# One row of w4 moved onto a part of the DMA engines, and the x row added on VectorE: a decode kernel on one core

## The chip, the cores and the metric

The kernel runs on one core of one Trainium2 chip. The metric is the device time in microseconds of one execution, the median of several runs. Beside the times there is one profiled execution, taken by the hardware profiler; its span runs from the first to the last instruction of the core and is about 2 us shorter than the time of the same execution.

## The reference, cut to what matters

```python
def _A_ref(x, k_cache, v_cache, wq, wo):           # x: 1 x 1 x 1024, already layer-normed
    q = (x @ wq) as 32 heads of 128
    k, v = 4 cached heads of 65536 keys x 128, each used by 8 query heads
    p = softmax(q k^T * 128 ** -0.5)
    return (p v) as one row of 4096 @ wo            # wo: 4096 x 1024

def _B_ref(x, w1, w2, w3, w4):
    h = gelu(layernorm(x) @ w1)
    hs = concatenate(four quarters of h, each shifted along the sequence) @ w2
    x1 = x + hs
    return x1 + gelu(layernorm(x1) @ w3) @ w4       # w3: 1024 x 3584, w4: 3584 x 1024

xn = layernorm(x)
return x + _A_ref(xn, ...) + _B_ref(xn, ...)
```

The sequence has one position, so every shifted quarter of h is zero; the kernel multiplies w2 with a column of zeros. All inputs are bf16. The two caches are 67 MB each; with the weights some 170 MB are read from HBM for one row of 1024 outputs.

## The kernel before, in words

Everything is a stream of loads through three large SBUF slots (`big`, 128 partitions x 64 KB, `SLOTS = 3`), and `Stream.pump` issues the next load on SyncE's queue (SP) as soon as a slot is free. The order is wq, w3, w1 and w2, then K and V in eight units (four cache heads, two halves each; the last V comes after wo), and at the end w4. A slot is free again when its user calls `st.done`.

For each unit `compute_k` transposes the K tile in place with VectorE (DVE, L361), multiplies it with the queries on TensorE (PE, L366), takes the maximum, lets ScalarE (ACT, L384) form the exponentials, and transposes these with DVE (L387). `compute_v` (L416) multiplies them with V. After the second unit of a cache head `group_rows` (L425 to L447) brings the heads' outputs into columns, and `project` multiplies them with wo.

The result is gathered in the PSUM tile `psB`: partitions 0-31 hold output columns 0 to 511, partitions 32-63 the other half, each row repeated 32 times. `row_acc` (L225) adds one product to it. Into `psB` go, in this order: the x terms (the x row scaled by `ln_s1` and shifted by `ln_s2`, as `accx`, through an identity), the w2 product, the projection of the first three heads (which `project` gathers in a row of PSUM, `copy_projection` at L463 copies to SBUF and `add_projection` adds through an identity), the products of w4 rows, and the projection of the last head.

w4 has 3584 rows, 28 for each partition; the tile `hT` holds in column c the 128 activations for row c of every partition. `W4_PIECES = (8, 12, 5, 2, 1)` gives the rows of each load (L187). The first 8 rows and the 12 of the second load go into `psB` with `compute_w4`: rows 0-2 at once, 3-7 behind the gathering of the last head, the 12 behind the last head's projection. Then ACT copies `psB` to `sums` (L497). The last `NARROW = 8` rows go, with output halves cut into quarters, to two other PSUM tiles (`pm_r`, L504): five rows (`AHEAD`), then `sums` through an identity, then three rows. ACT and DVE cast the two tiles (L520, L521), and ACT issues the store.

The lines around the change that a sentence doesn't say:

```python
copy_projection()
summed = compute_v(NU - 1)
with tc.issue_after(summed):
    add_projection()
early = sum(W4_PIECES[:AT_ONCE])
compute_w4(0, FIRST)
with tc.issue_after(tail["gathered"]):
    compute_w4(FIRST, early)
projected = project(HKV - 1)
with tc.issue_after(projected):
    compute_w4(early, FC - NARROW)
```

Of the kernel before, what the change touches and what calls it, by code (L numbers as in the profile page):

```python
# [8 lines left out]
BF16 = mybir.dt.bfloat16  # L9
F32 = mybir.dt.float32  # L10
ACTF = mybir.ActivationFunctionType
ALU = mybir.AluOpType
# [3 lines left out]
P = 128  # L16
# [3 lines left out]
SLOTS = 3  # L20
W4_PIECES = (8, 12, 5, 2, 1)
FIRST = 3
AT_ONCE = 1
NARROW = 8
AHEAD = 5

# [70 lines left out]
def kernel(  # L97
# [14 lines left out]
    nc = tc.nc  # L112
# [13 lines left out]
    assert DH == P and HQ // HKV == 8 and HKV == 4 and D == 1024 and F == 3584 and S == 1  # L126
    assert SK % UKEYS == 0 and sum(W4_PIECES) == FC
    NB = SK // UKEYS
# [22 lines left out]
    class Stream:  # L151
# [17 lines left out]
        def load(self, it):  # L169
            t = big.tile([P, ROW], BF16, name="big")  # L170
            self.tiles[it] = t
            go = nc.sync.dma_start
            if it == "wq":
                go(out=t[:], in_=A_wq.rearrange("(p c) n -> p (c n)", c=DC))
            elif it == "w3":
                go(out=t[:, 0:DC * F], in_=B_w3.rearrange("(p c) f -> p (c f)", c=DC))
            elif it == "w12":
                go(out=t[:, 0:DC * D], in_=B_w1.rearrange("(p c) n -> p (c n)", c=DC))
                go(out=t[:, DC * D:2 * DC * D], in_=B_w2.rearrange("(m c) n -> m (c n)", c=DC))
            elif it == "wo":  # L180
                go(out=t[:].rearrange("p (g n) -> p g n", g=HKV),
                   in_=A_wo.rearrange("(g p j) n -> p g (j n)", g=HKV, p=P))
            elif it == "w4":
                w4_v = B_w4.rearrange("(m c) n -> m c n", c=FC)
                c0 = 0
                for n in W4_PIECES:
                    go(out=t[:, c0 * D:(c0 + n) * D], in_=w4_v[:, c0:c0 + n, :].rearrange("p c n -> p (c n)"))  # L187
                    c0 += n
            else:
                kind, i = it  # L190
                g, b = divmod(i, NB)
                cache = A_k_cache if kind == "K" else A_v_cache
                go(out=t[:], in_=cache[0, g, b * UKEYS:(b + 1) * UKEYS, :].rearrange("(p ct) d -> p (ct d)", p=P))
# [18 lines left out]
    for b in range(2):  # L212
        nc.gpsimd.tensor_copy(
            out=spread[:, 2 * b:2 * b + 2, :].rearrange("p r (a i) -> p r a i", a=4),
            in_=ident_f[:, 64 * b:64 * b + 64].rearrange("p (i r) -> p r i", r=2).unsqueeze(2).to_broadcast([P, 2, 4, 32]))

    qdiag = const.tile([P, LEAD + 4 * P], BF16, name="qdiag")
    nc.gpsimd.memset(qdiag[:], 0.0)
# [5 lines left out]
    def row_acc(j, lhsT, rhs, start=False):  # L224
        return nc.tensor.matmul(psB[32 * j:32 * j + 32, :], lhsT=lhsT.to_broadcast([lhsT.shape[0], 32]), rhs=rhs, start=start,  # L225
                                stop=False, tile_position=(0, 32 * j), skip_group_check=True)
# [8 lines left out]
    def layernorm(src, tag):  # L235
# [44 lines left out]
    nc.vector.tensor_tensor(out=ln_s2[:], in0=negmean1[:], in1=rstd1[:], op=ALU.mult)  # L280
    accx = ppool.tile([1, D], F32, name="accx", tag="p")
    nc.vector.tensor_scalar(out=accx[:], in0=x_row[0:1, :], scalar1=ln_s1[0:1, 0:1], scalar2=ln_s2[0:1, 0:1],
                            op0=ALU.mult, op1=ALU.add)
    for j in range(2):
        row_acc(j, ident_f[0:1, 0:1], accx[0:1, 512 * j:512 * (j + 1)], start=True)

# [31 lines left out]

    hT = const.tile([P, FC], BF16, name="hT")

    def compute_w3():
# [8 lines left out]
        nc.vector.transpose(out=h_row[:], in_=h_row[:])  # L330
        nc.vector.tensor_copy(out=hT[:], in_=h_row[:, ::32])

    def compute_w12():
# [8 lines left out]
        for c in range(DC):  # L342
            for j in range(2):
                row_acc(j, g_col[:], wt[:, 1, c, 512 * j:512 * (j + 1)])
        st.done("w12")
# [115 lines left out]
    def copy_projection():  # L461
        tail["o"] = st.tiles["w4"][0:1, FC * D:FC * D + 2 * D].bitcast(F32)
        nc.vector.tensor_copy(out=tail["o"].rearrange("p (j n) -> p j n", j=2), in_=tail["rows"][0:1, 0:2, :])  # L463

    def add_projection():
        for j in range(2):
            row_acc(j, ident_f[0:1, 0:1], tail["o"][:, 512 * j:512 * (j + 1)])

# [7 lines left out]
    compute_w3()  # L476
    compute_w12()
    for u in range(NU - 1):
        compute_k(u)
        compute_v(u)  # L480
# [4 lines left out]
    copy_projection()  # L485
    summed = compute_v(NU - 1)
    with tc.issue_after(summed):
        add_projection()
    early = sum(W4_PIECES[:AT_ONCE])
# [4 lines left out]
    with tc.issue_after(projected):  # L494
        compute_w4(early, FC - NARROW)
    sums = ogpool.tile([64, 512], F32, name="sums", tag="og")
    nc.scalar.copy(out=sums[:], in_=psB[0:64, :])  # L497
    quarters = [ps_M.tile([P, 512], F32, name="pm_r", tag="pm") for _ in range(2)]
# [8 lines left out]
    def narrow_rows(lo, hi, start=False):  # L507
        wt = st.tiles["w4"]
        for c in range(lo, hi):
# [3 lines left out]

    narrow_rows(FC - NARROW, FC - NARROW + AHEAD, start=True)
    quarter_acc(lambda j: ident_f[0:64, 32 * j:32 * j + 1].to_broadcast([64, 32]),
                lambda j, h: sums[:, 256 * h:256 * (h + 1)])
    narrow_rows(FC - NARROW + AHEAD, FC)

# [34 lines left out]
```

## Time and profile before

| what | value |
|---|---|
| time, median of 7 runs | 400.90 us (400.78 to 401.01) |
| profiled execution: time, span | 400.86 us, 398.8 us |
| read from HBM | 169.87 MB, 426 GB/s over the span |
| busy: PE, DVE, ACT, GpSimd (POOL) | 230.8, 209.5, 27.6, 5.4 us |
| data queue (q1), share of 16 engines' span | 98.9% |
| w4's five loads issued on SP | 361.70 to 363.93 us of the span |
| last w4 load landed, last matmul begins | 396.60, 396.64 us |

The page of a profile gives busy time by engine, the granted TensorE clock and the DMA share in 40 slices, the DMA queues, and the chain of work that ended last. The chain and the timeline count microseconds from the start of the span. A line of the timeline has start, duration, engine, program line, operation, output and inputs with shapes, the count of merged instructions, and in brackets the idle time of the engine ahead of it with what ended it. Beside these views the trace keeps each DMA packet with its queue, start, duration and size, and each increment of a DMA's semaphore; it doesn't name the engine of a packet.

### The profile page before, as it was taken

How to read it: one execution, taken by the hardware profiler on the slowest of the kernel's cores; microseconds unless marked ns; L12 is line 12 of the kernel's file. 1: busy time of each engine (PE TensorE's matmuls, PEld its weight loads, DVE VectorE, ACT ScalarE, POOL GpSimd, SP SyncE). 2: the span in 40 equal slices, each digit the busy share in tenths (PEclk: the TensorE clock that was granted, in tenths of full speed). 3: DMA queues.
4: the chain of work that ended last, by engine and by line, in shares of the span. 5: the costliest groups of instructions: out<-in, count | busy, mean ns of one | idle time of the engine just before them, and what ended most of it. 6: DMA issues, size and time to landing. Idle time of an engine off the chain costs nothing.

```text
span 398.8 us, 2595 instructions
## 1 busy us (share of the span) xinstructions
PE 230.8 (58%) x1372; PEld 45.2 (11%) x878; DVE 209.5 (53%) x155; ACT 27.6 (7%) x36; POOL 5.4 (1%) x28
## 2 busy tenths in 40 slices
PE   0461960591569247833974286429543945394995
PEld 0210000000200110011001100101010102010132
DVE  0620010974196559643953696269449932894140
ACT  1001010003000200020002000200110010002000
POOL 2000000000000000000000000000000000000000
PEclk9996896697769587966695679678966886599999
DMA  9998999999999999999999999999999999999996
GB/s 421 421 443 380 440 440 480 440 421 421 416 428 427 421 480 442 421 421 427 427 429 427 460 454 416 421 421 434 440 429 447 447 427 388 417 450 442 406 428 254
DMA packets 4144, 170.03 MB, mean 426 GB/s; under 512 B 419, under 2 KB 421, under 8 KB 678
## 3 DMA queue, kind: packets, MB, share of 16 engines
q1 hardware_dynamic: 4128, 169.87, 98.9%
q8 instruction: 9, 0.15, 0.1%
q14 instruction: 1, 0.01, 0.0%
q10 hardware_dynamic: 6, 0.00, 0.0%
HBM read 169.87 MB, written 0.00 MB: 426 GB/s over the span
## 4 chain that ended last, share of the span: by engine, by line
DMA 56%; DVE 21%; PE 17%; ACT 2%; another core or an unknown queue 2%; issue 1%; SPq 0%; DVEq 0%; ACTq 0%
DMA big<-in_A_k_cache_dram 42%; DVE big L361 15%; PE sc L366 11%; DMA big<-in_B_w_dram 8%; DMA big<-in_A_wq_dram 5%; PE oacc L416 4%; DVE p_sb L387 2%; DVE mx L371 2%; ACT p_sb L384 2%; PE psq L291 1%; SPq L187 0%; PE pm_mx L373 0%; DVE m L375 0%; PE pm_mx L380 0%
## 5 line engine op out<-in xcount | busy, mean ns | idle before, releaser
L366 PE MATMUL sc<-big,qdiag 128*128 128x512 bf16 x512 | 130.5, 417 | 65.2 <-DVE big L361 59.5
L361 DVE STREAM_TRANSPOSE big<-big 128x4096 f32<-128x4096 f32 x32 | 139.4, 4412 | 50.5 <-DMA big<-in_A_k_cache_dram 50.5
L416 PE MATMUL oacc<-big,p_sb 128*32 128x512 bf16 x512 | 43.0, 510 | 34.5 <-DVE p_sb L387 34.5
L371 DVE TENSOR_REDUCE mx<-sc 128x1 f32<-128x2048 f32 x8 | 18.3, 2292 | 30.5 <-PE sc L366 30.5
L366 PEld LDWEIGHTS <-qdiag 128*128 128x128 bf16 x128 | 13.3, 104 | 177.9 <-issue 146.6
L384 ACT ACTIVATE p_sb<-sc,nball 128x2048 bf16<-128x2048 f32 x8 | 15.7, 1967 | 219.8 <-DVE nball L382 219.7
L387 DVE STREAM_TRANSPOSE p_sb<-p_sb 128x2048 bf16<-128x2048 bf16 x8 | 18.5, 2311 | 18.0 <-ACT p_sb L384 18.0
L416 PEld LDWEIGHTS <-p_sb 128*32 128x32 bf16 x512 | 16.7, 124 | 58.2 <-DVE p_sb L387 35.1
L291 PE MATMUL psh<-big,ln_rep_b 128*32 128x512 bf16 (+1 forms) x64 | 12.4, 941 | 8.5 <-DMA big<-in_B_w_dram 8.5
L373 PE MATMUL pm_mx<-ident_f,mx 128*1 128x128 f32 x8 | 2.3, 283 | 19.1 <-DVE mx L371 19.1
L456 PE MATMUL o_acc<-big,oT 128*1 128x512 bf16 x48 | 11.9, 412 | 2.4 <-ACT p_sb L384 2.4
L330 DVE STREAM_TRANSPOSE h_row<-h_row 128x896 bf16<-128x896 bf16 x1 | 1.1, 1111 | 21.6 <-ACT h_row L329 21.6
L425 DVE SCALAR_TENSOR_TENSOR og<-oacc,wb,og 128x512 f32<-128x512 f32 x4 | 3.0, 751 | 17.9 <-PE oacc L416 17.9
L239 PE MATMUL pm_ln<-ln_rowsum_a,ones_f 128*128 128x1 f32 x2 | 0.6, 348 | 12.7 <-DVE ln_rowsum_a L237 12.7
L438 PE MATMUL pm_e<-ol,sel8big 128*128 128x129 f32 x8 | 2.3, 370 | 8.5 <-DVE ol L437 8.5
L315 POOL COPY qdiag<-qx 32x32 bf16<-32x32 bf16 x16 | 3.3, 204 | 279.4 <-PE sc L366 250.5
L230 DVE STREAM_TRANSPOSE x_t<-x_row 32x256 bf16<-32x256 bf16 x4 | 2.5, 616 | 8.3 <-DMA x_row<-in_A_x_dram 8.3
L225 PE MATMUL psB<-big,hT 128*32 128x512 bf16 x40 | 4.8, 380 | 2.7 <-DMA big<-in_B_w_dram 2.7
L463 DVE COPY big<-o_acc 1x1024 f32<-1x1024 f32 x1 | 1.2, 1212 | 9.2 <-PE o_acc L456 9.2
L291 PE MATMUL psq<-big,ln_rep_a 128*32 128x512 bf16 x64 | 5.4, 511 | 1.0 <-DMA big<-in_A_wq_dram 1.0
L521 DVE CAST out_t<-pm_r 64x256 bf16<-64x256 f32 x1 | 0.4, 425 | 9.8 <-PE pm_r L504 9.8
L380 PE MATMUL pm_mx<-ident_f,rep 1*128 1x1 f32 x8 | 1.9, 240 | 5.0 <-DVE rep L377 5.0
(101 smaller groups left out, 76.4 us busy)
## 6 DMA issues: line engine op xcount, KB each, us to landing
big<-in_A_wo_dram SPq DMA_DIRECT2D x1, 8192.0 KB, 36.7
big<-in_B_w_dram SPq DMA_DIRECT2D x1, 7168.0 KB, 38.1
big<-in_B_w_dram SPq DMA_DIRECT2D x3, 2048.0 KB, 35.5
big<-in_B_w_dram SPq DMA_DIRECT2D x1, 3072.0 KB, 29.5
big<-in_B_w_dram SPq DMA_DIRECT2D x1, 1280.0 KB, 32.2
big<-in_B_w_dram SPq DMA_DIRECT2D x1, 512.0 KB
big<-in_B_w_dram SPq DMA_DIRECT2D x1, 256.0 KB, 33.1
big<-in_A_k_cache_dram SPq DMA_DIRECT2D x8, 41.8
```

The source lines that it names most:

```text
L225: return nc.tensor.matmul(psB[32 * j:32 * j + 32, :], lhsT=lhsT.to_broadcast([lhsT.shape[0], 32]), rhs=rhs, start=start, stop=False, tile_ ...
L230: nc.vector.transpose(out=x_t[32 * a:32 * a + 32].rearrange("p c j -> p (c j)"), in_=x_row[:, 256 * a:256 * (a + 1)].rearrange("p (i c) -> ...
L291: nc.tensor.matmul(acc[32 * q:32 * q + 32, i, 0:n], lhsT=rep[:, c, :], rhs=cols(c, i, q), start=(c == 0), stop=(c == DC - 1), tile_positio ...
L315: nc.gpsimd.tensor_copy(out=qdiag[at, LEAD:].rearrange("p (x c) -> p x c", x=4)[:, :, 32 * a:32 * a + 8], in_=qx[at, :, 8 * g:8 * g + 8])
L361: nc.vector.transpose(out=words, in_=words)
L366: nc.tensor.matmul(sc[:, e, :], lhsT=qdiag[:, c0:c0 + P], rhs=cols[:, s, e, :, b2, :, r], start=(s == 0 and b2 == 0 and r == 0), stop=(s = ...
L371: nc.vector.reduce_max(out=mx[:], in_=sc[:].rearrange("p e n -> p (e n)"), axis=AX.X)
L384: nc.scalar.activation(out=p_sb[:], in_=sc[:], func=ACTF.Exp, bias=nball[:, b:b + 1], scale=SCALE, accum_out=group["lall"][:, b:b + 1])
L387: nc.vector.transpose(out=flat, in_=flat)
L416: mm = nc.tensor.matmul(oacc[32 * q:32 * (q + 1), :], lhsT=pT[:, e, 32 * t:32 * (t + 1)], rhs=vt[:, :, e, t, :], start=(e == 0 and t < 4), ...
L425: nc.vector.scalar_tensor_tensor(out=og[:], in0=oacc[:], scalar=wb[:, 1:2], in1=og[:], op0=ALU.mult, op1=ALU.add)
L456: nc.tensor.matmul(tail["rows"][0:1, h2, :], lhsT=oT[g][:, j:j + 1], rhs=wt[:, g, j, 512 * h2:512 * (h2 + 1)], start=(g == 0 and j == 0), ...
```

## The change

The 28th row of each partition (row 27) is no longer loaded by a piece of its own into all 128 partitions. `W4_PIECES` becomes `(8, 12, 4, 2, 1)`, 27 rows, and the 128 rows that remain, of 2 KB each, are loaded by four further loads, issued behind the first piece, into three additional row places of the w4 tile (`SHARES`: k, rows per k, first partition, place). Their HBM sides begin with a dimension of 5, 5, 9 and 12, and they write 40, 40, 36 and 12 partitions, the third in steps of two and the fourth in steps of eight. Before them GpSimd fills these places, and a fourth one, with zeros.

The activations that belong to these rows must stand in the same partitions. GpSimd writes three 0/1 matrices (`place`) early in the kernel, `place_left` multiplies them with the column of the 28th activations on PE, and DVE copies the result to three more columns of `hT`. `compute_w4(WHOLE, WHOLE + 3)` adds the three columns' products to `psB` ahead of the 12-row piece.

The x terms no longer go through PE. DVE puts the two halves of x into partitions 0 and 32 (`x_halves`); late in the kernel it scales and shifts them into the fourth row place and adds the two rows of the projection; the sum is added to `psB` by DVE in place of ACT's copy. `add_projection` and the matmuls of `accx` go. The narrow rows become seven, four of them ahead of `sums`.

```diff
--- before.py
+++ after.py
@@ -18,11 +18,13 @@
 SUBS = 4
 SETS = 4
 SLOTS = 3
-W4_PIECES = (8, 12, 5, 2, 1)
+W4_PIECES = (8, 12, 4, 2, 1)
+SHARES = ((5, 8, 0, 0), (5, 8, 0, 1), (9, 4, 0, 2), (12, 1, 1, 2))
+WHOLE = 27
 FIRST = 3
 AT_ONCE = 1
-NARROW = 8
-AHEAD = 5
+NARROW = 7
+AHEAD = 4
 
 
 def keep_loaded_weights(nc):
@@ -124,7 +126,7 @@
     FC = F // P
     UKEYS = P * ROW // DH
     assert DH == P and HQ // HKV == 8 and HKV == 4 and D == 1024 and F == 3584 and S == 1
-    assert SK % UKEYS == 0 and sum(W4_PIECES) == FC
+    assert SK % UKEYS == 0 and sum(W4_PIECES) == WHOLE == FC - 1
     NB = SK // UKEYS
     NU = HKV * NB
     SCALE = float(DH) ** -0.5
@@ -182,10 +184,18 @@
                    in_=A_wo.rearrange("(g p j) n -> p g (j n)", g=HKV, p=P))
             elif it == "w4":
                 w4_v = B_w4.rearrange("(m c) n -> m c n", c=FC)
+                nc.gpsimd.memset(t[:, WHOLE * D:(WHOLE + 4) * D].bitcast(F32), 0.0)
                 c0 = 0
                 for n in W4_PIECES:
                     go(out=t[:, c0 * D:(c0 + n) * D], in_=w4_v[:, c0:c0 + n, :].rearrange("p c n -> p (c n)"))
                     c0 += n
+                    if c0 == n:
+                        m0 = 0
+                        for k, m, i0, x in SHARES:
+                            go(out=t[i0:8 * k:8 // m, (WHOLE + x) * D:(WHOLE + x + 1) * D],
+                               in_=w4_v[m0:m0 + k * m, WHOLE, :].rearrange("(i e) n -> e i n", e=k))
+                            m0 += k * m
+                        assert m0 == P
             else:
                 kind, i = it
                 g, b = divmod(i, NB)
@@ -214,6 +224,8 @@
             out=spread[:, 2 * b:2 * b + 2, :].rearrange("p r (a i) -> p r a i", a=4),
             in_=ident_f[:, 64 * b:64 * b + 64].rearrange("p (i r) -> p r i", r=2).unsqueeze(2).to_broadcast([P, 2, 4, 32]))
 
+    x_halves = const.tile([64, 512], BF16, name="x_halves")
+    nc.gpsimd.memset(x_halves[:], 0.0)
     qdiag = const.tile([P, LEAD + 4 * P], BF16, name="qdiag")
     nc.gpsimd.memset(qdiag[:], 0.0)
     g_col = const.tile([P, 1], BF16, name="g_col")
@@ -278,11 +290,16 @@
     nc.vector.tensor_scalar(out=ln_s1[:], in0=rstd1[:], scalar1=1.0, scalar2=None, op0=ALU.add)
     ln_s2 = const.tile([P, 1], F32, name="ln_s2")
     nc.vector.tensor_tensor(out=ln_s2[:], in0=negmean1[:], in1=rstd1[:], op=ALU.mult)
-    accx = ppool.tile([1, D], F32, name="accx", tag="p")
-    nc.vector.tensor_scalar(out=accx[:], in0=x_row[0:1, :], scalar1=ln_s1[0:1, 0:1], scalar2=ln_s2[0:1, 0:1],
-                            op0=ALU.mult, op1=ALU.add)
     for j in range(2):
-        row_acc(j, ident_f[0:1, 0:1], accx[0:1, 512 * j:512 * (j + 1)], start=True)
+        nc.vector.tensor_copy(out=x_halves[32 * j:32 * j + 1, :], in_=x_row[0:1, 512 * j:512 * (j + 1)])
+    place = ogpool.tile([P, 3, 16, 8], BF16, name="place", tag="og")
+    nc.gpsimd.memset(place[:], 0.0)
+    m0 = 0
+    for k, m, i0, x in SHARES:
+        cells = place[:, x, 0:k, i0::8 // m]
+        nc.gpsimd.affine_select(out=cells, in_=cells, compare_op=ALU.not_equal, fill=1.0, base=-m0,
+                                pattern=[[-1, k], [-k, m]], channel_multiplier=1)
+        m0 += k * m
 
     def row_matmul(acc, rep, cols, widths):
         for c in range(DC):
@@ -316,7 +333,8 @@
                 out=qdiag[at, LEAD:].rearrange("p (x c) -> p x c", x=4)[:, :, 32 * a:32 * a + 8],
                 in_=qx[at, :, 8 * g:8 * g + 8])
 
-    hT = const.tile([P, FC], BF16, name="hT")
+    hT = const.tile([P, WHOLE + 3], BF16, name="hT")
+    h_left = const.tile([P, 1], BF16, name="h_left")
 
     def compute_w3():
         wt = st.tiles["w3"][:, 0:DC * F].rearrange("p (c m k) -> p c k m", c=DC, k=FC)
@@ -328,7 +346,15 @@
         nc.scalar.activation(out=h_row[:, 0:512], in_=psh[:, 0, :], func=ACTF.Gelu_apprx_tanh)
         nc.scalar.activation(out=h_row[:, 512:], in_=psh[:, 1, 0:32 * FC - 512], func=ACTF.Gelu_apprx_tanh)
         nc.vector.transpose(out=h_row[:], in_=h_row[:])
-        nc.vector.tensor_copy(out=hT[:], in_=h_row[:, ::32])
+        nc.vector.tensor_copy(out=hT[:, 0:WHOLE], in_=h_row[:, 0:32 * WHOLE:32])
+        nc.vector.tensor_copy(out=h_left[:], in_=h_row[:, 32 * WHOLE:32 * WHOLE + 1])
+
+    def place_left():
+        pm = ps_M.tile([P, 512], F32, name="pm_h", tag="pm")
+        for x in range(3):
+            nc.tensor.matmul(pm[:, x:x + 1], lhsT=place[:, x].rearrange("p e i -> p (e i)"), rhs=h_left[:],
+                             start=True, stop=True)
+        nc.vector.tensor_copy(out=hT[:, WHOLE:], in_=pm[:, 0:3])
 
     def compute_w12():
         wt = st.tiles["w12"][:, 0:2 * DC * D].rearrange("p (w c n) -> p w c n", w=2, c=DC)
@@ -341,7 +367,7 @@
         nc.scalar.activation(out=h1[:], in_=ps1[0:32, 0:2, :], func=ACTF.Gelu_apprx_tanh)
         for c in range(DC):
             for j in range(2):
-                row_acc(j, g_col[:], wt[:, 1, c, 512 * j:512 * (j + 1)])
+                row_acc(j, g_col[:], wt[:, 1, c, 512 * j:512 * (j + 1)], start=(c == 0))
         st.done("w12")
 
     group = {}
@@ -459,12 +485,12 @@
         return mm.ins if g == HKV - 1 else None
 
     def copy_projection():
-        tail["o"] = st.tiles["w4"][0:1, FC * D:FC * D + 2 * D].bitcast(F32)
-        nc.vector.tensor_copy(out=tail["o"].rearrange("p (j n) -> p j n", j=2), in_=tail["rows"][0:1, 0:2, :])
-
-    def add_projection():
+        tail["o"] = st.tiles["w4"][:, (WHOLE + 3) * D:(WHOLE + 4) * D].bitcast(F32)
+        nc.vector.tensor_scalar(out=tail["o"][0:64, :], in0=x_halves[:], scalar1=ln_s1[0:64, 0:1], scalar2=ln_s2[0:64, 0:1],
+                                op0=ALU.mult, op1=ALU.add)
         for j in range(2):
-            row_acc(j, ident_f[0:1, 0:1], tail["o"][:, 512 * j:512 * (j + 1)])
+            row = tail["o"][32 * j:32 * j + 1, :]
+            nc.vector.tensor_tensor(out=row, in0=tail["rows"][0:1, j, :], in1=row, op=ALU.add)
 
     def compute_w4(lo, hi):
         wt = st.tiles["w4"]
@@ -475,6 +501,7 @@
     compute_wq()
     compute_w3()
     compute_w12()
+    place_left()
     for u in range(NU - 1):
         compute_k(u)
         compute_v(u)
@@ -483,18 +510,17 @@
     for g in range(HKV - 1):
         project(g)
     copy_projection()
-    summed = compute_v(NU - 1)
-    with tc.issue_after(summed):
-        add_projection()
+    compute_v(NU - 1)
     early = sum(W4_PIECES[:AT_ONCE])
     compute_w4(0, FIRST)
     with tc.issue_after(tail["gathered"]):
         compute_w4(FIRST, early)
     projected = project(HKV - 1)
     with tc.issue_after(projected):
-        compute_w4(early, FC - NARROW)
+        compute_w4(WHOLE, WHOLE + 3)
+        compute_w4(early, WHOLE - NARROW)
     sums = ogpool.tile([64, 512], F32, name="sums", tag="og")
-    nc.scalar.copy(out=sums[:], in_=psB[0:64, :])
+    nc.vector.tensor_tensor(out=sums[:], in0=psB[0:64, :], in1=tail["o"][0:64, :], op=ALU.add)
     quarters = [ps_M.tile([P, 512], F32, name="pm_r", tag="pm") for _ in range(2)]
 
     def quarter_acc(lhsT, rhs, start=False):
@@ -511,10 +537,10 @@
                         lambda j, h: wt[:, D * c + 512 * j + 256 * h:D * c + 512 * j + 256 * (h + 1)],
                         start=start and c == lo)
 
-    narrow_rows(FC - NARROW, FC - NARROW + AHEAD, start=True)
+    narrow_rows(WHOLE - NARROW, WHOLE - NARROW + AHEAD, start=True)
     quarter_acc(lambda j: ident_f[0:64, 32 * j:32 * j + 1].to_broadcast([64, 32]),
                 lambda j, h: sums[:, 256 * h:256 * (h + 1)])
-    narrow_rows(FC - NARROW + AHEAD, FC)
+    narrow_rows(WHOLE - NARROW + AHEAD, WHOLE)
 
     out_t = ogpool.tile([64, 2, 256], BF16, name="out_t", tag="og")
     nc.scalar.copy(out=out_t[:, 0, :], in_=quarters[0][0:64, 0:256])
```

## The prediction

> **What bounds the kernel.** I read the page's slices and queues first, then the chain in order of time, then the timeline of the last 20 us, and last the records of single DMA packets. A difference of 0.2% is 0.80 us here, about what a measurement of this kernel can tell from no change.
>
> ```profile
> DMA  9998999999999999999999999999999999999996
> ...
> q1 hardware_dynamic: 4128, 169.87, 98.9%
> q8 instruction: 9, 0.15, 0.1%
> ```
>
> The 16 DMA engines are full from the first slice to the last but one. All 169.87 MB are still to be moved after the change, so only the tail and the spread between the engines can move the time. Queue q8 is to be noted: nine packets of 16 KB that are not data.
>
> The chain in order of time (start, us, what) ends thus:
>
> ```profile
> 363.50 33.10 DMA big<-in_B_w_dram
> 396.60 0.04 issue
> 396.64 0.34 PE pm_r L504 x4
> 396.98 0.02 issue
> 397.01 0.42 DVE out_t L521
> ```
>
> The end waits for w4's last piece, landed at 396.60, then needs four matmuls, a cast and the store. The timeline (start, us, engine, line, what) shows how far behind the other work stands:
>
> ```profile
> 379.46 1.21 DVE L463 COPY big<-o_acc 1x1024 f32<-1x1024 f32 x1 [9.15 <-PE o_acc L456]
> ...
> 383.01 1.05 PE L225 MATMUL psB<-big,ident_f 1*32 1x512 f32 x4
> 383.13 0.75 DVE L425 SCALAR_TENSOR_TENSOR og<-oacc,wb,og 128x512 f32<-128x512 f32 x1 [2.46 <-PE oacc L416]
> 383.92 0.69 DVE L436 TENSOR_TENSOR og<-og,mask 128x512 f32<-128x512 f32 x1
> ...
> 391.65 2.77 PE L225 MATMUL psB<-big,hT 128*32 128x512 bf16 x24 [2.46 <-DMA big<-in_B_w_dram]
> 394.45 0.58 ACT L497 COPY sums<-psB 64x512 f32<-64x512 f32 x1 [26.75 <-PE psB L225]
> ...
> 395.42 0.64 PE L504 MATMUL pm_r<-sums,ident_f 64*32 64x256 f32 x8
> ```
>
> PE waits 2.46 us for the 12-row piece. After it PE has its own chain (24 wide matmuls, the copy of psB, eight matmuls of sums, narrow rows), which is ready for the last row at 396.40, only 0.24 us before the DMA. A DMA that ends earlier meets this second bound quickly.
>
> The packet records give the spread. A packet starts 3 to 4 ns before the one ahead of it on its engine ends, so the packets can be threaded into 16 chains. The last packets of piece 1 end at 394.06 to 394.56 on seven engines and at 395.48 to 396.17 on nine. The landing comes 0.43 us later. At the V landing near 107 us fourteen engines still stood within 0.54 us of each other; each late engine lost its time in one stretch, eight of them to a q8 packet (1.02 to 1.09 us, and the data packet beside it takes 0.5 to 0.65 us longer) and one to an 8 KB packet of q14. Seven engines thus idle 1.5 us at the end.
>
> [...] the one-row x load has a single 2 KB packet. It lies on a chain that is early (end 394.36)[...]. [...]
>
> **The loads.** [...] Rows of 2 KB per engine: engines 0-4 get 8+8+4+1 = 21, 5-8 get 4+1 = 5, 9-11 get 1, 12-15 none; before, each had 8. A 2 KB packet takes 84 ns and starts 80 ns after the last, so 21 rows are 1.7 us and 5 rows 0.4 us. Without its eight rows an engine would end where piece 2 ended: about 393.4 to 393.9 (early) and 394.8 to 395.5 (late). If engines 0-4 are early they now end at 395.1 to 395.6; the worst late engine ends at 395.5 with none or one row, 395.9 with five. Landing (+0.43) is 396.0 to 396.35 instead of 396.60.
>
> **PE's chain to the last row.** The 12-row piece has 20 rows before its end as before, and the shares as well: it lands at about 391.6 with a late engine of 0 or 1 row, 392.0 with one of five. The 24 matmuls stay: end 394.42 to 394.8. The psB add is now on DVE, priced by L436 (0.69, same 512 elements) against ACT's 0.58: sums at 395.15 and, with the handover, matmuls from 395.2 (before 395.42, since 20 narrow matmuls stood ahead and waited for their piece till 394.76; now there are 16 and theirs lands near 394.1). Plus 0.57 for the sums and two rows of 0.11: row 26 can start at 396.0 to 396.4 (before 396.64). The later of both bounds is 396.0 to 396.42, a gain of 0.2 to 0.65; I take 0.4.
>
> **The rest, priced at nothing with its cover.**
> - GpSimd's zeroing of four row places (128x2048 f32): from 128x128 f32 at 0.20 and 128x1 at 0.10, some 1.7 us; by qdiag's 536 elements in 0.55, 2.1. SP has issued piece 8 and holds the shares and four pieces behind that wait; nine issues at about 0.45 end by 368. The first engine finishes piece 8 at 381.75, so the cover is 13 us.
> - copy_projection: one DVE copy of 1.21 becomes a scale-and-shift (L397's like shape 0.45) and two adds (0.69 each by L436): 1.83 from 379.46, done by 381.3, before L425 at 383.13. Were that cover gone, PE's 2.46 hole takes the next.
> - The four matmuls of add_projection (1.05 at 383.01) go; PE then waits for piece 8 (384.30) all the same. No gain.
> - The six matmuls on the shares' three columns (0.69 by 24 in 2.77) fit into the 2.46 hole from 389.19; the shares land near 384.5.
> - At the start: PE loses four x matmuls[...] that ended before wq landed at 21.97; DVE swaps 0.80 for two half copies; GpSimd adds a few small fills in an idle time of 28 us. After w12: three matmuls and two tiny DVE copies, where PE idles 16 us. All under the DMA; were it not, at most 1 us of them would show.
>
> **Sum.** The profiled execution took 400.86 with a span of 398.8; 0.4 less is 400.46. The median is 0.04 above that execution: 400.5.
>
> **Rivals.**
> 1. [...] In full lockstep their 21 rows take 1.7 us more; they end at 396.8 to 397.3 against 396.17, the time is 401.5 to 402.0. It decides from about 0.6 us of such loss. [...] Half the loss would give 401.0 at most. [...] Chance 0.17.
> 2. The lower engines are not the early ones. [...] A late engine with 21 rows ends at 396.5 to 397.2: 401.2 to 401.9. Chance 0.20.
> 3. PE is the bound, or landing is no earlier because an engine of 5-8 is the latest one: 400.7 to 400.9, no change. Chance 0.15.
> 4. The last q8 packet. It came at 395.97 just as PE ended the sums. [...] if it comes half a microsecond earlier on an engine with rows left, that engine loses 1.5 us: 401.6. Chance 0.05.
>
> **Chances.** The main case, a gain of 0.2 to 0.65, has 0.43. No case that I can work out reaches 0.8 us of gain, since the worst late engine without any row allows 0.65; I leave 0.06. Slower by over 0.2% is over 401.7: half of rivals 1, 2 and 4, and something for what I don't see, 0.24. Within: 0.70. The range runs from the best sum, 400.2, to 401.7.
>
> **What would show it.** Right: piece 12 lands at 391.6 to 392.0, the four share loads between 383 and 385, the engines' last ends within 0.8 us of each other instead of 2.1, the last four pm_r matmuls at 396.0 to 396.4. Wrong: share packets well over 84 ns[...], a group of chains that end after 396.5 (wrong engines), a q8 packet between 394 and 396, or a last row that waits for PE's own sums and not for a landing.

## The result and the profile after

The changed kernel takes 402.95 us in the median (402.12 to 404.16), the kernel before 400.84 in the same comparison. The ratio is 1.0055 (95% interval 1.0045 to 1.0065): slower by 2.1 us in the medians, outside the forecast range of 400.2 to 401.7 and on the side that the forecast gave 0.24. The profiled execution of the changed kernel took 404.08 us with a span of 401.9 us, so it is one of the longer ones; the shorter ones are returned to below. Of the 2.1 us some 0.2 lie outside the span: time less span is 2.14 to 2.25 us in the executions of the changed kernel, and 1.95 to 2.14 in those of the kernel before that were timed beside its repeat.

The end of the chain in order of time, changed kernel (start, us, what):

```profile
366.86 26.85 DMA big<-in_B_w_dram
393.71 0.04 issue
393.76 4.12 PE psB L237 x20
...
397.88 0.34 PE psB L237 x2
398.22 0.02 issue
398.25 0.69 DVE sums L523
398.94 0.04 issue
398.99 1.13 PE pm_r L530 x20
400.12 0.02 issue
400.14 0.43 DVE out_t L547
```

Before, the chain went from the last landing (396.60) straight to the last four matmuls. Now it goes from the landing of the 12-row piece (393.71) through `psB`, the add on DVE and `sums`. The last row landed at 398.09 and had nobody waiting for it. TensorE's own chain has become the bound, and it starts 2.1 us later than before: that piece landed at 391.61.

The same stretch, landing to complete `psB`, in both kernels (window, its length, busy time and count for PE, PEld, DVE, ACT and POOL, then granted clock, DMA share, GB/s); first the kernel before, then the changed one:

```profile
391.60:394.45 2.85, 2.77 (x24) 1.24 (x23) 0.00 (x0) 0.00 (x0) 0.00 (x0) 1.00 0.94 384
```

```profile
393.70:398.25 4.55, 4.49 (x37) 2.10 (x38) 0.00 (x1) 0.00 (x0) 0.00 (x0) 0.62 0.50 200
```

The clock column, the third from the end, is to be read here. The 24 wide matmuls are the same, but at a mean granted clock of 0.62 they take 1.7 us longer (4.50 from landing to end against 2.81). The granted clock was 0.5 from 394.31 to 397.72; before, such a stretch began at 397.61, behind the last matmul. The clock accounts for all of it: 3.41 us at half clock do the work of 1.7, and 4.50 less 1.7 is 2.8, the duration before.

The rest of the sum is 0.67 us given back: from a complete `psB` to the end of the last matmul it is 1.84 us (398.22 to 400.06) against 2.51 (394.42 to 396.93), because no landing is waited for any more. 2.10 + 1.69 - 0.67 = 3.12 us, which is the difference of the two spans.

Threading the packets by engine, as the prediction did, tells where the 2.10 comes from. "Shares" are the packets of the four additional loads; "hit" means that a packet of q8 or q14, which carries no data of the kernel, delayed the engine. The counts of 2 KB packets (21 in five chains, 5 in four, 1 in three, 0 in four, as forecast) give each chain its group of engines: those that take part in most of the loads are called 0 to 4, and so on. Ends in us of piece 8, of the shares, of the 12-row piece, and of the last packet, in the changed kernel:

```
engines   hit by                 piece 8         shares          12-row piece     last
0-4       four without a hit     381.69-382.08   383.83-384.30   391.61-392.02    396.01-396.42
0-4       one, q14 at 113.4      383.47          385.74          393.24           397.63
5-8       one, q8 at 335.9       384.47          385.01          392.59           396.98
5-8       one, q8 at 383.4       381.77          382.19          391.65           396.05
5-8       two without a hit      381.87, 381.99  382.29, 382.41  390.81, 390.55   395.21, 394.96
9-11      three, q8              383.69-383.99   383.81-384.08   391.58-391.78    395.97-396.17
12-15     three, q8              383.85-384.08   -               391.59-391.75    395.99-396.14
12-15     one without a hit      381.97          -               390.11           394.53
```

One engine is alone at the end: the one of engines 0 to 4 that lost some 1.2 us to the 8 KB packet at 113 us and then was given 13 rows more than before. Also the shares' packets took 107.7 ns in the mean (up to 176) where the prediction measured 84 for such packets, and the 24 KB packets of the 12-row piece 984 ns against 920.

### The profile page after: what moved, and what is told of

Its sections match the earlier page's. It is cut to its first block, busy times and chain, and to the rows that moved or that the text cites. A ratio compares the mean times of both kernels' runs of the same rounds, so it can differ in the third digit from the quotient of the medians.

```text
span 401.9 us, 2615 instructions
## 1 busy us (share of the span) xinstructions
PE 227.8 (57%) x1369; PEld 45.3 (11%) x875; DVE 210.8 (52%) x161; ACT 27.1 (7%) x35; POOL 9.0 (2%) x35
## 3 DMA queue, kind: packets, MB, share of 16 engines
q1 hardware_dynamic: 4287, 169.87, 98.4%
## 4 chain that ended last, share of the span: by engine, by line
DMA 54%; DVE 21%; PE 19%; ACT 2%; another core or an unknown queue 2%; SPq 1%; issue 1%; POOLq 0%; DVEq 0%; ACTq 0%
DMA big<-in_A_k_cache_dram 42%; DVE big L387 15%; PE sc L392 11%; DMA big<-in_B_w_dram 7%; DMA big<-in_A_wq_dram 5%; PE oacc L442 4%; DVE p_sb L413 2%; DVE mx L397 2%; ACT p_sb L410 2%; PE psq L308 1%; PE psB L237 1%; SPq L195 1%; POOLq L574 0%; ACT L410 0%
## 5 line engine op out<-in xcount | busy, mean ns | idle before, releaser
L392 PE MATMUL sc<-big,qdiag 128*128 128x512 bf16 x512 | 128.7, 411 | 65.5 <-DVE big L387 65.3
L442 PE MATMUL oacc<-big,p_sb 128*32 128x512 bf16 x512 | 44.3, 522 | 34.5 <-DVE p_sb L413 34.5
L237 PE MATMUL psB<-big,hT 128*32 128x512 bf16 x46 | 7.3, 467 | 5.6 <-DMA big<-in_B_w_dram 5.6
```

The costliest lines, as they stand in the source:

```text
L392: nc.tensor.matmul(sc[:, e, :], lhsT=qdiag[:, c0:c0 + P], rhs=cols[:, s, e, :, b2, :, r], start=(s == 0 and b2 == 0 and r == 0), stop=(s = ...
L442: mm = nc.tensor.matmul(oacc[32 * q:32 * (q + 1), :], lhsT=pT[:, e, 32 * t:32 * (t + 1)], rhs=vt[:, :, e, t, :], start=(e == 0 and t < 4), ...
```

## The experiments

Theory A: one of the five lower engines is late, and its rows make it the last. Theory B: the partitions that the additional rows are written to slow the packets. In the changed kernel the rows of one index e of a load's first dimension lie in a block of eight partitions, 8e to 8e+7 ("blocks of eight" below); in the second run they lie in 4e to 4e+3 and 32+4e to 32+4e+3, and in its last load in 64+4e ("blocks of four"). Theory C: TensorE's low-clock stretch takes most of the loss. They don't exclude each other, so each kernel takes one away or isolates it. A theory D, on why the clock falls, came later and has its own two kernels at the end.

### The changed kernel again

No edit.

> The changed kernel again, unchanged, as the yardstick of this set. Theory A (one of engines 0 to 4 is late, so its 13 additional rows make it the last) and theory B[...] both expect the loads to end as in the first profile: 12-row piece landed near 393.7, last landing near 398.1. Theory C (a low-clock stretch of TensorE that falls on the psB matmuls is most of the loss) expects the time to differ between executions by about 1.7 us, according to where the stretch falls, with the landings where they were: 402.2 without it, 404 with it.

Measured: 403.23 us, ratio 1.0059 (1.0045 to 1.0072). Its six times fall into two groups, 402.06 to 402.71 and 403.76 to 403.93; so do the twelve of the result, where six lie at or below 402.66 and the others at 403.24 or above. The profile, of an execution of 403.76, has the landings of the first (393.61 and 397.97) and again a low-clock stretch (394.78 to 398.20) on the psB matmuls:

```profile
393.65 3.39 PE L237 MATMUL psB<-big,hT 128*32 128x512 bf16 x20 [3.32 <-DMA big<-in_B_w_dram]
396.79 0.67 PE L237 MATMUL psB<-big,hT 128*32 128x512 bf16 x2
397.22 0.67 PE L237 MATMUL psB<-big,hT 128*32 128x512 bf16 x2
397.93 0.68 DVE L523 TENSOR_TENSOR sums<-psB,big 64x512 f32<-64x512 f32 x1 [8.92 <-PE psB L237]
```

The bracket of the first line shows that PE had been idle for 3.32 us, waiting for the piece. The landings repeat to 0.12 us. The two groups of times lie some 1.5 us apart, about what the low clock costs the psB matmuls in the two profiles (1.5 and 1.7 us). Both profiles are of the longer group, so that the shorter one had no stretch there is not seen in them; the runs with TensorE's idle time filled test it.

### Blocks of four: the same rows on the same engines, in other partitions

```diff
-SHARES = ((5, 8, 0, 0), (5, 8, 0, 1), (9, 4, 0, 2), (12, 1, 1, 2))
+SHARES = ((5, 4, 0, 1, 0), (5, 4, 32, 1, 0), (5, 4, 0, 1, 1), (5, 4, 32, 1, 1), (9, 4, 0, 1, 2), (12, 1, 64, 4, 2))
+# k, rows per k, first partition, step, place; place's cells follow the same partitions
```

> The same 128 rows on the same engines in the same numbers (21, 5, 1, 0), but [...] in six loads. Theory A alone: packets fall to 84 ns, but the late one of engines 0 to 4 still has 13 rows more: its last packet ends near 396.5 instead of 397.6, the 12-row piece lands near 392.6 instead of 393.7; about 401.3 to 401.9 without a low-clock stretch. Theory B alone: both landings fall to 391.6 and 396.1, 400.5. [...]

Measured: 401.69 us, ratio 1.0031 (1.0019 to 1.0043); four of the six times are 401.57 to 401.77. Share packets fell to 88.3 ns in the mean, the 12-row piece landed at 392.78 and the last row at 397.15. That is theory A's forecast within 0.2 us on both landings. Four of engines 0 to 4 end their last packet at 395.36 to 395.62, the fifth, hit by q14 at 113.4, at 396.69. For this one engine:

```
                 piece 8   shares   12-row piece   last
before           383.17    -        390.47         395.48
blocks of four   383.15    384.95   392.31         396.69
changed kernel   383.47    385.74   393.24         397.63
```

The rows alone cost it 1.21 us (13 rows at 81 ns are 1.05), the blocks of eight 0.94 more. A and B are each about half of the late landing. The profiled execution (403.3 us) met a low-clock stretch too, so its span isn't a price of A. The four short times are 0.8 to 1.0 above the kernel before, but their spans (399.0 to 399.1 us) only 0.3 to 0.4; the rest lies outside the span and is returned to with the version below.

### Even rows: everything but the distribution

```diff
-SHARES = ((5, 8, 0, 0), (5, 8, 0, 1), (9, 4, 0, 2), (12, 1, 1, 2))
+SHARES = ((128, 1, 0, 0),)
-    go(out=t[i0:8 * k:8 // m, ...], in_=w4_v[m0:m0 + k * m, WHOLE, :].rearrange("(i e) n -> e i n", e=k))
+    go(out=t[:, ...], in_=w4_v[:, WHOLE, :])
```

> The 28th row goes in one ordinary load of 128 partitions at the same place in the queue (8 rows for every engine); all else is as in the changed kernel, VectorE's x included. Theories A and B: the last landing is that of before, 396.6, and the 12-row piece lands 0.65 later than before because one row stands ahead of it; 400.9 to 401.3. If the x on VectorE, the zero fill or the added matmuls were the cause: still 402 or more.

Measured: 400.85 us, ratio 1.0002 (0.9994 to 1.0010). The x on VectorE, the zero fill, the placing of the activations and the three additional columns cost nothing that can be measured; the whole loss lies in how the row's 128 parts are distributed. The 12-row piece landed at 391.96 and the last at 396.33:

```profile
392.00 2.77 PE L236 MATMUL psB<-big,hT 128*32 128x512 bf16 x24 [1.34 <-DMA big<-in_B_w_dram]
394.80 0.68 DVE L522 TENSOR_TENSOR sums<-psB,big 64x512 f32<-64x512 f32 x1 [6.75 <-PE psB L236]
395.54 0.64 PE L529 MATMUL pm_r<-sums,ident_f 64*32 64x256 f32 x8 [0.34 <-DVE sums L522]
396.11 0.56 PE L529 MATMUL pm_r<-big,hT 128*32 128x256 bf16 x12
```

These four lines follow each other with the predicted prices at full clock. The last matmuls run on from `sums` without a gap: landing and TensorE's chain are level.

### Naming the engines, twice

```diff
+                for k in range(1, 16):
+                    c0 = 2 * DC * D + 384 * k
+                    go(out=t[0:k, c0:c0 + 384], in_=B_w4[0:k, 0:384])
```

> The kernel before with 15 additional loads of 768 bytes a partition behind w2, into 1 to 15 partitions of an unused part of that slot, so that engine e carries 15 - e small packets and each chain of packets can be named. The time has no meaning here. Theory A: one of engines 0 to 4, not engine 0, carries the 8 KB q14 packet near 113 us, and eight others, all from engine 5 up, carry a 16 KB q8 packet. Theory B alone: engines 0 to 4 carry none.

This one (407.84 us) told nothing: the 15 loads stood together in SP's queue, and the chains of packets could not be followed past them. The second form puts one load behind each of 15 K and V loads of the kernel before:

```diff
+                if self.mark < 15:
+                    self.mark += 1
+                    go(out=marks[0:self.mark, :], in_=B_w4[0:self.mark, 0:384])
```

> The kernel before with one small load (768 bytes a partition, into 1 to 15 partitions of a scratch tile) behind each of the first 15 K and V loads, so that engine e carries 15 - e small packets while its queue never runs dry, and each chain of packets can be named. The time is of no interest (401 to 402). Theory A: exactly one of engines 1 to 4 is late, by the 8 KB q14 packet near 113 us; the eight others that are late by a q8 packet are all numbered 5 or higher. Theory B alone: engines 0 to 4 are all early.

The execution took 401.22 us, and all 16 chains can be followed to their end; an engine's number is 15 less the count of small packets in its chain. q14's 8 KB packet, here at 103.5 us, runs on engine 3. The q8 packets from 42 us on run on engines 12, 13, 14, 5, 6, 9, 8, 11 and again 8: all from 5 up, as theory A expects. Untouched are 0, 1, 2, 4, 7, 10 and 15, seven engines, as many as end early in the kernel before. In the changed kernel and with blocks of four it is likewise one of engines 0 to 4 that carries q14's packet; that it is engine 3 there too is inferred. Which of the upper engines a q8 packet takes differs from program to program: the one near 198 us is on engine 5 here, on one of 12 to 15 in the changed kernel, on one of 9 to 11 with blocks of four.

### Even rows in blocks of eight

```diff
-SHARES = ((5, 8, 0, 0), (5, 8, 0, 1), (9, 4, 0, 2), (12, 1, 1, 2))
+SHARES = ((16, 8, 0, 0),)
```

> The 28th row in one load that gives every engine eight rows (no imbalance), but as the changed kernel places them[...]. Theory B: share packets take well over 84 ns, and the engines in the 8- and 12-row pieces beside them are slowed; the early engines lose some of their lead but the late ones little, 401.0 to 401.4. Theory A alone[...]: packets at 84 ns, the time of the even kernel with its ordinary load, 400.85.

Measured: 403.58 us, ratio 1.0066 (1.0047 to 1.0084), with one time of 401.93 and five from 403.23 to 404.62, far above what even theory B expected. Eight rows for every engine, as in the even kernel; only the partitions differ. Share packets take 112.0 ns in the mean (even kernel 84.4), 24 KB packets 979 ns (922), and the 12-row piece lands at 393.07 instead of 391.96, the last row at 397.43 instead of 396.33. So the placement alone makes the landing 1.1 us later. The HBM side of the load is split as with blocks of four, whose packets took 88 ns, so it isn't that. The rest is again the clock, in this profile down to 0.5 from 394.24 to 397.65:

```profile
393.11 3.16 PE psB L237 x19
...
397.40 0.69 DVE sums L523
```

### A late landing and nothing else

```diff
-    go(out=t[:, (WHOLE + x) * D:(WHOLE + x + 1) * D], in_=w4_v[:, WHOLE, :])
+    for x in range(3):
+        go(out=t[:, (WHOLE + x) * D:(WHOLE + x + 1) * D], in_=w4_v[:, WHOLE, :])
```

> The even kernel with the load of the 28th row three times (the second and third meet activations of zero): 16 more rows of 2 KB on every engine, no imbalance[...]. Each engine is 1.3 us later, so the 12-row piece lands near 393.2 instead of 391.96 and the last near 397.6. If a late landing costs only itself: 402.1 to 402.2 in every execution. Theory C (TensorE's low-clock stretch then meets the psB matmuls, whatever made the landing late): executions of 402.1 beside others near 403.7, as with the changed kernel, and a profile in which the psB matmuls take over 4 us from the landing instead of 2.8.

Measured: 404.08 us, ratio 1.0079 (1.0059 to 1.0100), with six times of 402.07, 402.16, 403.72, 404.44, 404.52 and 405.02. The profile is of the second, and its tail is at full clock:

```profile
393.40:396.20 2.80, 2.77 (x34) 1.50 (x37) 0.00 (x0) 0.00 (x0) 0.00 (x0) 1.00 0.90 364
```

The piece landed at 393.39 and psB was complete 2.81 us later, as before the change; the low-clock stretch had come at 386.93. Two executions cost just the later landing (1.2 to 1.3 us over the even kernel), as forecast for them. The other four took 1.6 to 2.9 more; by their spans (401.2 to 402.3 us against 399.9 and 400.0) it is 1.2 to 2.4, since two of them also took 3.2 and 3.7 us outside the span. No engine has more rows than another here, and the rows come in ordinary loads of 128 partitions. Theory C holds in this form: in executions whose 12-row piece lands at 392.8 us or later, a low-clock stretch often falls on the psB matmuls, whatever made them late. In the 13 executions of the even kernel, whose piece lands at 391.96, none is above 401.08. That the four longer ones had the stretch on these matmuls is inferred from the other profiles; they have no trace. Why a late landing should bring the low clock is tested two sections below.

### A version from the findings, and its control

```diff
-W4_PIECES = (8, 12, 4, 2, 1)
-SHARES = ((5, 8, 0, 0), (5, 8, 0, 1), (9, 4, 0, 2), (12, 1, 1, 2))
+W4_PIECES = (8, 11, 5, 2, 1)
+SHARES = ((3, 4, 0, 1, 0), (3, 4, 0, 1, 1), (3, 4, 32, 1, 1), (3, 4, 0, 1, 2), (16, 4, 32, 1, 0), (16, 1, 32, 4, 2))
-NARROW = 7
-AHEAD = 4
+NARROW = 8
+AHEAD = 5
```

> A version drawn from the experiments: additional rows only for engines 0 to 2, which the map shows early in the kernel before[...] (21 rows), 5 rows for every other engine; and the pieces are 8, 11, 5, 2, 1, so that psB is complete earlier. Theory A with B: the late engines carry three rows less (0.24 us), the last landing is near 396.35 instead of 396.6, the 11-row piece lands near 391.4: 400.5 to 400.65. If other engines are late in this program, or the idle lead can't be used at all: 400.85 or more.

The control is the even kernel with the same pieces.

> The control for the version: even rows in one ordinary load, with the pieces 8, 11, 5, 2, 1. The last landing bounds it as before: 400.8 to 400.9. If TensorE's chain behind the 12-row piece was the bound and not the landing, it is faster than the even kernel by up to 0.2.

Measured: 400.99 us, ratio 1.0003 (0.9996 to 1.0011) for the version, 400.91 us, ratio 1.0001 (0.9993 to 1.0009) for the control. Neither beats the kernel before. In the trace the version does what it was drawn for: its last row landed at 396.27 (forecast 396.35, before 396.60) and the chain ends as it did before, at a landing:

```profile
385.05 11.22 DMA big<-in_B_w_dram
396.27 0.04 issue
396.31 0.34 PE pm_r L530 x4
396.65 0.02 issue
396.68 0.43 DVE out_t L547
```

The 0.33 us arrive in the span but not in the time. The version's 13 spans are 398.3 to 398.8 us with a median of 398.5, those of the kernel before and of the control have a median of 398.7. Outside the span, however, 11 of the 13 executions took 2.45 to 2.65 us, and none of the kernel before in the same comparison over 2.12. Blocks of four, the other kernel with six share loads, took 2.50 to 2.67 there and once 3.34; the other changed kernels took 2.13 to 2.27, but for two executions each of the late landing and of the even rows in blocks of eight. So with six share loads, as far as these two kernels show, something is added outside the span; what fills that time was not tried.

### TensorE's idle time filled

Theory D was the author's estimate after the runs above: the later landing lengthens TensorE's idle time ahead of the 12-row piece, and idle time is what lowers the clock. In the changed kernel's profile the clock was at 0.5 for 3.41 us, from 394.31, and before that PE had nothing at all to do until the landing (windows, columns as above):

```profile
390.48:393.72 3.24, 0.00 (x0) 0.00 (x0) 0.00 (x0) 0.00 (x0) 0.00 (x0) 1.00 0.96 402
```

Two kernels fill this time with matmuls that nobody reads, into an unused part of a PSUM tile: 12 in the changed kernel, 8 in the late landing.

```diff
         compute_w4(WHOLE, WHOLE + 3)
+        for _ in range(12):        # 8 in the late landing
+            nc.tensor.matmul(tail["rows"][0:32, 2, :], lhsT=hT[:, 0:1].to_broadcast([P, 32]), rhs=st.tiles["w4"][:, 0:512],
+                             start=True, stop=True, tile_position=(0, 0))
         compute_w4(early, WHOLE - NARROW)
```

> The changed kernel with 12 additional 128x512 matmuls on rows already loaded, into an unused part of PSUM, behind the shares' columns and ahead of the 12-row piece: TensorE's idle time of 3.3 us before that piece is filled to within about 0.7 us. Theory D: the low-clock stretch follows from that idle time; then it is gone from the psB matmuls, all executions fall into the lower group, 402.0 to 402.7, and psB is complete 2.8 us after the landing at 393.7. If the stretch comes from anything else (the late start itself, or work already done): the times keep their two groups, up to 404.

> The kernel with the late landing and nothing else, with 8 such matmuls in the same place, which fills 1.7 us of the 2.8 us for which TensorE would wait at full clock. Theory D: most executions at 402.0 to 402.3 and the upper group (403.7 to 405.0) gone or rare. Otherwise: both groups as without the filling.

Measured: the changed kernel, filled, takes 402.32 us, ratio 1.0038 (1.0025 to 1.0050), with five times from 402.13 to 402.75. The late landing, filled, takes 402.15 us, ratio 1.0032 (1.0020 to 1.0045), with six times from 402.01 to 402.27. The longer group is gone from both, although the piece lands nearly as late as without the filling (393.42 and 393.32, against 393.71 and 393.39). The repeat of the changed kernel and the late landing were timed on other chips; on the chip of the filled kernels the even rows in blocks of eight had five of six times in the longer group, so the chip alone doesn't explain it. The changed kernel, filled, in the trace's timeline (start, us, engine, operation; in brackets the idle time before it):

```profile
389.61 0.81 PE L237 MATMUL psB<-big,hT 128*32 128x512 bf16 x6
390.26 2.75 PE L522 MATMUL o_acc<-big,hT 128*32 128x512 bf16 x12
393.46 2.77 PE L237 MATMUL psB<-big,hT 128*32 128x512 bf16 x24 [0.45 <-DMA big<-in_B_w_dram]
```

and the late landing, filled:

```profile
393.36 2.77 PE L237 MATMUL psB<-big,hT 128*32 128x512 bf16 x24 [1.31 <-DMA big<-in_B_w_dram]
```

PE does 12 matmuls more and is done sooner: the same 24 matmuls are back at 2.77 us, with 0.45 or 1.31 us of idle time ahead of them and no longer 3.3 as in the changed kernel. The late landing's own profile, at full clock without any filling, fits as well: there an earlier stretch, from 386.93, had made PE slow, so that it was busy until 392.57 and idle for 0.86 us only. Theory D holds: with the landing left late and the idle time gone, the loss to the clock is gone. The filled kernel also shows what remains without the low clock: its span is 399.9 us, 1.1 above the kernel before, and its last row landed at 397.78, 1.18 later than before. That is the price of the late landing alone.

The length of the wait alone doesn't decide. The kernel with blocks of four had a stretch behind 2.39 us of idle time, while the kernel before shows none behind 2.46. The clock's changes in the traces give the missing part: full and half clock both last whole multiples of 3.41 us (in the kernel before full clock 1 to 6 times that, half clock 1 to 4 times, up to the last stretch), so that a profile can be cut into steps of this length, counted back from a change. The step ahead of, or across, the start of the psB matmuls (for the late landing the one ahead of its earlier stretch), with PE's busy time in it:

```
run                      step              PE busy    clock after it
changed kernel           390.90-394.31     0.55       half
the changed one again    391.37-394.78     1.13       half
even, blocks of eight    390.82-394.24     1.13       half
blocks of four           389.16-392.57     1.27       half
late landing             383.51-386.93     1.50       half
before                   387.37-390.78     1.82       full
before                   390.78-394.20     2.55       full
even rows                389.74-393.15     2.07       full
changed kernel, filled   391.58-395.00     2.97       full
late landing, filled     389.05-392.46     3.00       full
```

A boundary at 390.78 divides the 2.46 us of the kernel before, and each part leaves its step enough work; 2.1 of the 2.39 us with blocks of four fall into one step. The same holds over the whole of twelve profiles (all but that of the first naming of the engines). Of the steps at full clock that end before the kernel's last matmul, 208 have under 1.4 us of matmuls, and the clock fell after each of them; it fell after one of the 11 with 1.4 to 1.5 us, and after none of the 536 with more. So a step need not be idle throughout: the clock fell behind steps with up to 1.4 us of work. Where the steps lie differs between executions (one begins at 390.90 in the one profile of the changed kernel and at 391.37 in the other), and that fits one kernel having two groups of times. Of the timed executions of the kernel before a few in each comparison took 401.3 to 401.9; whether those met a stretch isn't known.

## Why the prediction was wrong

**The bound.** Right: all data is to be moved anyway, the spread of the engines is the lever, and a second bound (the 12-row piece, psB, sums) stands close behind the landing. The second one became the bound: the end waited for PE's sums, 2.10 us late by the landing and 1.69 by the clock, and not for the last row.

**The step that failed first** is "If engines 0-4 are early", from which the last engine was to end at 395.1 to 395.9. Four of five were early; the fifth ended at 397.63. The prediction had read from the same packet records that one late engine was hit by q14 and not by q8, but could name no engine; that the early chain with the x row's packet is engine 0 was the author's estimate. Rival 2 held the right case, at 0.20.

**The price of a packet.** 84 ns was taken for the shares; the engine that ends last needed 2.27 us for its 21 rows where 1.7 was reckoned, and its 8-row and 12-row pieces were slowed beside them. Rival 1 held this, at 0.17: in blocks of eight 112 ns, in blocks of four 88, with the same bytes. Its size, an estimate, was wrong: it put up to 1.7 us more on engines 0 and 4, in lockstep. That didn't occur, and the loss wasn't confined to that pair: all five took 2.14 to 2.36 us for their 21 rows, against 1.79 to 1.93 with blocks of four. The runs show that the placement makes the difference; by what way the partitions slow the packets was not shown. The share loads landed at 386.15 to 386.66, forecast near 384.5, still ahead of their matmuls at 389.67.

**Rivals that add up.** Each rival was priced with the other at zero and capped at 402.0. Both held, on the same engine: +1.21 and +0.94. The range left their sum out.

**TensorE's chain at full clock.** The landing of the 12-row piece was given as 391.6 to 392.0 and psB as 2.77 us after it. At 393.7 the matmuls met the low clock in both profiles of the changed kernel, 1.5 to 1.7 us that no case contained. The prediction followed what waits for the piece, and left out what the waiting does to PE itself: 3.28 us of idle time instead of 2.46, which left 0.55 us of work in a step of 3.41, and the clock came down.

**The sum as it stands.** Of the 18 executions of the changed kernel (the result's twelve and the repeat's six) nine took 402.06 to 402.71 and nine 403.24 to 404.16. The first nine, some 1.6 us above the kernel before in the median, and the filled kernel, 1.5 above, carry the late landing, about half of it rows on the late engine and half their blocks of eight, and some 0.2 us outside the span. The other nine carry some 1.5 us more. The median of 402.95 lies between the groups and is the time of neither.

**What was priced at nothing.** Right, by the even kernel. Two details differ without cost. DVE did the scale and the adds not at 379.46 but among the last head's steps:

```profile
386.90 0.39 DVE L469 TENSOR_REDUCE o<-msk 128x8 f32<-128x128 f32 x1
387.20 0.53 DVE L489 TENSOR_SCALAR big<-x_halves,ln_s,ln_s 64x512 f32<-64x512 bf16 x1
387.66 0.22 DVE L473 TENSOR_SCALAR oT<-o,rl 128x8 bf16<-128x8 f32 x1
387.79 1.36 DVE L493 TENSOR_TENSOR big<-o_acc,big 1x512 f32<-1x512 f32 x2
```

oT, which the last projection waits for, is thereby some 0.3 us later (0.76 us after the start of the reduction, before 0.42), under PE's wait for the 12-row piece. And SP's queue didn't end by 368: two of the last pieces waited for earlier loads,

```profile
SPq L190 <- DMA big<-in_A_v_cache_dram: 11.4, 1, 11.4
SPq L190 <- DMA big<-in_B_w_dram: 5.6, 1, 5.6
```

and the last was issued at 385.27. On the engines the packets follow one another past that time, most starting 3 to 4 ns before the one ahead ends, so this cost nothing here.

**The last q8 packet** (rival 4) did not fall between the rows: none starts after 383.42 in the profile of the changed kernel. Before, they came 172 to 343 recorded instructions of PE and its weight loads apart, 259 in the mean.

## What to carry to other kernels

Before rows are moved to engines that "are early", name the engines: a few small loads of 1 to 15 partitions mark each chain of packets, and the lateness must be read for the engine that gets the rows, not for their average. Try the placement of the rows, too: in blocks of eight partitions they cost 1.1 us at the landing here, and the second run's blocks of four brought the packets from 108 ns to 88. And where a landing moves later, look at what its consumers meet there, the granted clock above all: 1.3 us of delay became 2.5 to 3.6 us of the span in four of six executions, because TensorE, with too little to do while it waits, then meets half clock, which in these profiles came behind every full-clock step of 3.41 us with under 1.4 us of work. Where it would do so little ahead of a burst that the end depends on, give it something to do: 12 matmuls for nobody removed the longer group, which was half of the executions and took 1.5 us more.

## What the runs showed of the hardware

- A 2 KB load packet takes 84 ns in the mean in the ordinary load of the even kernel, and 108 (changed kernel, up to 176) to 112 (even rows) in loads that lay the rows in blocks of eight partitions; the large packets beside it are slowed too (984 against 920 ns for 24 KB). In blocks of four, with the same bytes, it takes 88.
- One 8 KB q14 packet puts its engine some 1.2 us behind (blocks of four: last packet at 396.69 against 395.36 to 395.62), one 16 KB q8 packet some 1.5 to 1.6 (changed kernel, engines 12 to 15: 395.99 to 396.14 against 394.53). It keeps this to the end; the data queue fills 98.4% of the engines' span in these two profiles. q14's packet (at 113.4 us in the changed kernel and with blocks of four, at 103.5 in the naming run) fell on one of engines 0 to 4 in every program whose chains could be named, q8's on engines 5 and up.
- In these traces TensorE's stretches of half clock last 3.41 us or multiples of it, and so do those of full clock between them. Full clock ended, up to the last matmul of a kernel, after every such step with under 1.4 us of matmuls (208 steps) and after none with over 1.5 (536). With 3.3 us of idle time ahead of 24 matmuls in the profiles of the changed kernel, half of its executions were of the longer group, in the late landing four of six; with that time filled by 12 or 8 matmuls, none of 11.
